# Sketched attention and SwiGLU on one core: one chunk made plain, one weight third differenced later, two chunks summed on VectorE

## The chip, the cores and the metric

One core of one Trainium2 chip runs the whole program. The metric is the time of one execution in microseconds; the kernel before was run three times. TensorE, VectorE, ScalarE, GpSimd and SyncE are PE, DVE, ACT, POOL and SP in the profile; "PEld" is TensorE's weight loading, which overlaps its products. Each engine, and each engine's queue of DMA issues, works strictly in the order in which the program lists its instructions.

## What is computed

```
phi(x) = outer product of (S1 x) and (S2 x), 8 x 8 = 64 features      q, k, v: 4 batches x 4 heads x 1088 x 32
num = phi(q) . sum_s phi(k) v^T        den = phi(q) . sum_s phi(k) + 1e-6
x = num / den, heads side by side                                     4352 tokens x 128
g = x @ w_gate;  val = x @ w_val;  out = (silu(g) * val) @ w_out      d_ff = 1536, in 12 chunks of 128
```

## The kernel before, in words

**Tiles.** The tokens stand as columns (`xT`, 128 x 4352) and are cut into blocks: three of 384, 320 and 384 columns for the first batch, and then `line`, the seven later blocks 3 to 9: six of 480 columns and a last one of 384. A *unit* is one block with one of the 12 chunks of d_ff: the products with `w_gate` and `w_val`, the Silu, and the product of the two, which gives a "hidden" tile. After that the unit's hidden tile is multiplied by its chunk of `w_out` and added up over the chunks in PSUM (`down`).

**The later blocks.** The loop over `y` (L1427) runs through 84 units; unit `y` is chunk `y % 12` of block `line[y // 12]`. Below, (m, j) is chunk j of `line[m]`, so unit 12 is (1, 0) and unit 26 is (2, 2). In each turn of the loop `start_unit` is called for unit y+1 (L1006: two matmuls into a pair of PSUM banks, and L1009: ACT rescales the pair), then `finish_unit` for unit y (L1018 and L1019: four more matmuls into its pair; L1021: ACT's Silu; L1026: DVE's multiply, which writes the hidden tile and gives the pair of banks back), and then `down` for an older unit. There are three pairs, so the start of unit y+3 cannot write the second bank of its pair until L1026 of unit y has read it.

**Plain and fine chunks.** `down` has two forms. A *plain* chunk is one fp32 matmul (L1094), which the profile shows as two passes. A *fine* chunk, listed in `DOWN` (L904), is three fp32r matmuls (L1086, L1088, L1089) with three parts of the hidden tile, `h1`, `h0` and `hd`, and three parts of `w_out`, `w1`, `wb` and `wd` (the tile `dparts`). `cut_hidden` (L960) makes the parts of the hidden tile: `h1` a scaled and rounded copy (ACT, L975, one unit later), `h0` the rest (DVE, L983, two units later), `hd` their sum. For a *carried* chunk `hd` is made by DMA: SP copies `h1` into it (L977) and POOL issues a DMA that adds `h0` to it (L987). For the others DVE adds (L989). All chunks of `line[:3]` in `DOWN` are carried; of the blocks 6 to 8 the odd ones; of the last none. The parts live in sets of three buffers, taken from a list and given back by `down`.

**The parts of w_out.** `cut_down` (L925) makes `dparts` in three thirds of the ten chunks 1 to 10: a is chunks 1 to 3, b is 4 to 6, c is 7 to 10. DVE's last step, `differ` (L941), gives `wd`; for c it is queued behind unit 12. Only L1086 reads `wd`.

**Order by hand.** `add_to(before, y, f)` and `add_to(behind, y, f)` put a step into the program ahead of unit y's four finishing matmuls, or behind its L1026. Nothing is rescheduled afterwards. The list `mine` (L1079) holds a block's fine chunks; behind the last of them `copy_out` (L1107) lets ACT copy the fine sums out of PSUM (L1112) into one of the five `sg` buffers; `put_together` adds both sums (L1122), and `store` transposes them (L1146) for the output.

**Attention of the later batches** is spread over the same units. Around units 9 to 19 it is batch 2's query step: DVE's L382 (last key features, tile `late`), L757, L760, L762, L763 and L764 (the denominators), then L382 and L774 in turn; POOL's five adds L552 (`zs`, the sums of the key features), which read what L382 wrote; SP's small copies L742; ACT's loads L178. POOL also makes `x0` of the next block (L884).

Of the kernel before, what the change touches and what calls it, by code (L numbers as in the profile page):

```python
# [19 lines left out]
def kernel(  # L20
# [53 lines left out]
    LAST = len(blocks) - 1  # L74
# [758 lines left out]
    def whole(ap):  # L833
        return ap.bitcast(FP32)
# [66 lines left out]

    line = list(range(HEAD, len(blocks)))
    FINE = range(1, NCH - 1)
    DOWN = [(line[0], j) for j in (2, 3, 4, 5, 6, 9)]  # L904
    DOWN += [(line[1], j) for j in (6, 7, 8, 9, 10)]
    DOWN += [(line[2], j) for j in (1, 2, 4, 5, 6, 8, 9, 10)]
    DOWN += [(i, j) for i in line[3:6] for j in FINE]
    DOWN += [(LAST, j) for j in range(1, 9)]
    down_parts = {}
# [6 lines left out]
    before, behind = {}, {}  # L916

    def add_to(where, y, f):
        where.setdefault(y, []).append(f)

    def now(where, y):
        for f in where.pop(y, ()):
            f()

    def cut_down():  # L925

        n = len(FINE)
        parts = const.tile([P, 3, n, D], F32R, tag="room", name="dparts", bufs=1)
        w1, wb, wd = (parts[:, k] for k in range(3))
        down_parts.update(w1=w1, wb=wb, wd=wd)  # L930

        def high(c):
            nc.scalar.activation(w1[:, c], wo[:, FINE[0] :][:, c], AF.Copy, scale=CUT)

        def left(c):
            nc.gpsimd.tensor_tensor(
                out=wb[:, c], in0=whole(w1[:, c]), in1=wo[:, FINE[0] :][:, c], op=ALU.subtract
            )

        def differ(c):  # L940
            nc.vector.scalar_tensor_tensor(  # L941
                out=wd[:, c], in0=whole(wb[:, c]), scalar=BETA, in1=whole(w1[:, c]),
                op0=ALU.mult, op1=ALU.add,
            )

        a, b, c = slice(0, 3), slice(3, 6), slice(6, n)
        high(a)
        yield
        high(b)
        yield  # L950
        high(c)
        add_to(behind, 2, lambda: left(a))
        add_to(behind, 2, lambda: left(b))
        add_to(behind, 5, lambda: differ(a))
        add_to(behind, 6, lambda: differ(b))
        add_to(behind, 2, lambda: left(c))
        add_to(behind, 12, lambda: differ(c))
        yield

    def cut_hidden(y, i, j):  # L960

        while len(h_free) < 3:
            y0, tags = h_more.pop(0)
            assert y >= y0
            for tag, n in tags:
                t = const.tile([P, n, WB], F32R, tag=tag, name="h" + tag, bufs=1)
                h_free.extend(t[:, k, :] for k in range(n))
        n = SPLIT if i == LAST else blocks[i][1]
        h_sets[i, j] = [h_free.pop(0) for _ in range(3)]
        h1, h0, hd = h_parts[i, j] = [x[:, 0:n] for x in h_sets[i, j]]  # L970
        h = hidden[i, j][:, 0:n]
        small = -CUT / BETA
        carried = i in line[:3] or i != LAST and j % 2
        if carried or j % 2:
            add_to(behind, y + 1, lambda: nc.scalar.activation(h1, h, AF.Copy, scale=small))  # L975
        if carried:
            add_to(behind, y + 1, lambda: nc.sync.dma_start(out=whole(hd), in_=whole(h1)))  # L977
        if not carried and j % 2 == 0:
            high = lambda: nc.vector.tensor_scalar(h1, h, small, None, op0=ALU.mult)
            before.setdefault(y + 1, []).insert(0, high)  # L980

        def rest():
            nc.vector.scalar_tensor_tensor(  # L983
                out=h0, in0=whole(h1), scalar=BETA, in1=h, op0=ALU.mult, op1=ALU.add
            )
            if carried:
                nc.gpsimd.dma_start(out=hd, in_=h0, accum_op=ALU.add)  # L987
            else:
                nc.vector.tensor_tensor(out=hd, in0=whole(h1), in1=whole(h0), op=ALU.add)  # L989

        add_to(before, y + 2, rest)
# [19 lines left out]
    def finish_unit(i, j, y=None):  # L1011
        n = blocks[i][1]
        x1, x0, _ = (x[:, 0:n] for x in x_parts[i])
        ps = sums_of.pop((i, j))
        now(before, y)
        for k, w in enumerate((wg, wv)):
            w1, wb = (w_parts[id(w), j // 3][t][:, j % 3, :] for t in range(2))
            nc.tensor.matmul(ps[:, k], w1, x1, start=False, stop=False, skip_group_check=True)  # L1018
            nc.tensor.matmul(ps[:, k], wb, x0, start=False, stop=True, skip_group_check=True)  # L1019
        sg = fpool.tile([P, WB], FP32, tag="sg", name="sg", bufs=5)[:, 0:n]  # L1020
        nc.scalar.activation(sg, ps[:, 0], AF.Silu, scale=WHOLE)  # L1021
        slot_of[i, j] = slots.pop(0)
        hj = slot_of[i, j]
        hidden[i, j] = hj
        todo.append((i, j))
        nc.vector.scalar_tensor_tensor(  # L1026
            out=hj[:, 0:n], in0=ps[:, 1], scalar=WHOLE, in1=sg, op0=ALU.mult, op1=ALU.mult
        )
        let_go((i, j))
        now(behind, y)  # L1030
        if (i, j) in DOWN:
            cut_hidden(y, i, j)
# [38 lines left out]
    def down(y=None):  # L1071
# [6 lines left out]
        made[i] = made.get(i, 0) + 1  # L1078
        mine = [c for c in range(NCH) if (i, c) in DOWN]  # L1079
        if mine and j == mine[0]:  # L1080
# [129 lines left out]
    c0, c1, aside = fpieces  # L1210
# [188 lines left out]
    while todo:  # L1399
        if len(todo) == 2:  # L1400
            start_unit(HEAD, 0)
        next_down()
        at(*steps_at.get(len(todo), ()))
        next(x_steps, None)
        if len(todo) == 7:
            parts_of(1)
            x_steps = cut_tokens(HEAD, nc.vector, soon=True)
            next(x_steps)
        if len(todo) == 6:
            down_steps = cut_down()  # L1410
        if len(todo) in (4, 5, 6):
            next(down_steps, None)
        if len(todo) in (2, 3, 4):
            parts_of(1)
# [77 lines left out]
```

## Time and profile before

| what | value |
|---|---|
| time of the kernel before, median of 3 runs | 276.21 us (275.74 to 276.25) |
| the profiled execution's own time | 276.19 us |
| its span, from first to last instruction | 274.5 us (1.69 us of the time lies around it) |
| DVE busy | 221.1 us (81%) |
| ACT busy | 197.6 us (72%) |
| POOL busy | 85.7 us (31%) |
| granted TensorE clock | 1.0 |
| DMA moved | 31.03 MB, mean 113 GB/s |

A row of the timeline gives the start and the duration in us, engine, line, operation, tiles and shape, and in brackets how long the engine had been idle before it and what released it. A row of the chain of waits gives start, duration, and the engine or DMA that held the end up in that stretch. In a table of windows each engine's busy time in the stretch is given, then the granted clock, the busy share of the DMA engines and GB/s.

### The profile page before, as it was taken

The page shows a single profiled execution, that of the slowest core. Times are in us where ns is not written, and L with a number is a line of the kernel's source. Part 1 is how long each engine was busy: PE and PEld are TensorE (multiplying, and loading weights), DVE is VectorE, ACT ScalarE, POOL GpSimd, SP SyncE. Part 2 cuts the span into 40 slices and gives each one's busy share as a digit, 9 for nine tenths or more (in the row PEclk, how much of TensorE's full clock was granted, in tenths as well). Part 3 has the DMA queues.
Part 4 walks back from the last instruction along what each step waited for, and adds up shares of the span by engine and source line. Part 5 has one row for each costly group of instructions (what it writes and reads, how often), then busy time and mean ns, then how long its engine had stood idle before and what let it go on. Part 6 is the DMA issues. An engine that isn't in the chain of part 4 may idle for free.

```text
span 274.5 us, 5978 instructions
## 1 busy us (share of the span) xinstructions
PE 266.5 (97%) x2208; PEld 203.1 (74%) x2208; DVE 221.1 (81%) x423; ACT 197.6 (72%) x353; POOL 85.7 (31%) x108
## 2 busy tenths in 40 slices
PE   7899999999999999998999999999999999999994
PEld 6645566666785777876677878767888888789994
DVE  3997988989788798999766788668968986996981
ACT  2468666462686789866678998768979888897860
POOL 3313422149340593273042143313213221221000
PEclk9999999999999999999999999999999999999999
DMA  6573197121331057751137688954464472565021
GB/s 194 169 218 89 46 264 207 61 104 56 68 87 24 4 145 184 150 132 31 38 90 174 124 203 170 193 109 108 91 121 114 101 160 63 125 125 110 2 36 30
DMA packets 35933, 31.03 MB, mean 113 GB/s; under 512 B 20928, under 2 KB 33984, under 8 KB 35904
## 3 DMA queue, kind: packets, MB, share of 16 engines
q1 hardware_dynamic: 29776, 21.64, 27.7%
q0 software_dynamic: 4896, 8.36, 17.8%
q10 hardware_dynamic: 1232, 0.66, 0.9%
q8 instruction: 17, 0.28, 0.4%
q14 instruction: 12, 0.10, 0.1%
HBM read 11.41 MB, written 2.23 MB: 50 GB/s over the span
## 4 chain that ended last, share of the span: by engine, by line
PE 86%; DVE 6%; DMA 3%; ACT 2%; issue 1%; ACTq 0%; SPq 0%
PE PS L1094 15%; PE PS L1006 13%; PE PS L1018 13%; PE PS L1019 12%; PE PS L1042 12%; PE PS L1086 4%; PE PS L1089 4%; PE PS L1088 4%; PE PS L359 2%; PE PS L347 2%; DMA hkT<-hextra 2%; PE PS L792 2%; PE PS L393 2%; DMA kld<-in_k_dram 2%; DVE hbuf L1026 1%
## 5 line engine op out<-in xcount | busy, mean ns | idle before, releaser
L1009 ACT ACTIVATE PS<-PS 128x960 f32<-128x960 f32 (+1 forms) x90 | 83.3, 925 | 26.7 <-PE PS L1006 25.9
L1026 DVE SCALAR_TENSOR_TENSOR hbuf<-PS,sg 128x480 f32<-128x480 f32 (+1 forms) x81 | 51.9, 640 | 25.8 <-ACT sg L1021 23.2
L1021 ACT ACTIVATE sg<-PS 128x480 f32<-128x480 f32 (+1 forms) x90 | 49.7, 552 | 2.2 <-PE PS L1019 1.9
L1094 PE MATMUL PS<-hbuf,wo 128*128 128x480 f32 (+3 forms) x88 | 36.9, 510 | 0.0
L1006 PE MATMUL PS<-xd,wd 128*128 128x480 f32 (+1 forms) x90 | 33.7, 375 | 1.0 <-DVE hbuf L1026 1.0
L1006 PE MATMUL PS<-xd,graw 128*128 128x480 f32 (+1 forms) x69 | 34.1, 494 | 0.0
L1019 PE MATMUL PS<-x,wb 128*128 128x480 f32 (+1 forms) x90 | 33.5, 372 | 0.0
L1018 PE MATMUL PS<-x,w 128*128 128x480 f32 (+1 forms) x90 | 33.4, 371 | 0.0
L1019 PE MATMUL PS<-x,graw 128*128 128x480 f32 (+1 forms) x69 | 25.6, 371 | 0.0
L1042 PE MATMUL PS<-xT,wg 128*128 128x384 f32 (+1 forms) x60 | 23.5, 473 | 0.1
L1042 PE MATMUL PS<-xT,wv 128*128 128x384 f32 (+1 forms) x60 | 23.2, 468 | 0.3 <-DVE wv L288 0.3
L1006 PEld LDWEIGHTS PS<-xd,wd 128*128 128x128 f32 x90 | 16.9, 188 | 8.5 <-issue 2.1
L1046 ACT ACTIVATE sg<-PS 128x384 f32<-128x384 f32 (+1 forms) x24 | 11.2, 468 | 13.1 <-PE PS L1042 12.3
L1094 PEld LDWEIGHTS PS<-hbuf,wo 128*128 128x128 f32 x88 | 16.3, 189 | 4.0 <-issue 0.4
L1018 PEld LDWEIGHTS PS<-x,w 128*128 128x128 f32 x90 | 16.9, 188 | 2.2
L1019 PEld LDWEIGHTS PS<-x,wb 128*128 128x128 f32 x90 | 16.9, 188 | 2.1
L1018 PE MATMUL PS<-x,graw 128*128 128x480 f32 (+1 forms) x48 | 18.0, 376 | 0.0
L1006 PEld LDWEIGHTS PS<-xd,graw 128*128 128x128 f32 x69 | 13.0, 188 | 6.1 <-ACT PS L1009 2.6
L1042 PEld LDWEIGHTS PS<-xT,wv 128*128 128x128 f32 x60 | 11.2, 190 | 7.4 <-DVE hbuf L1057 0.8
L1042 PEld LDWEIGHTS PS<-xT,wg 128*128 128x128 f32 x60 | 10.9, 190 | 7.7 <-issue 1.1
L1018 PE MATMUL PS<-x,gphq 128*128 128x480 f32 (+1 forms) x42 | 16.0, 380 | 0.1
L1019 PEld LDWEIGHTS PS<-x,graw 128*128 128x128 f32 x69 | 12.9, 188 | 1.4
(287 smaller groups left out, 576.3 us busy)
## 6 DMA issues: line engine op xcount, KB each, us to landing
kld<-in_k_dram SPq DMA_DIRECT2D x4, 544.0 KB, 4.3
qld<-in_q_dram SPq DMA_DIRECT2D x3, 544.0 KB, 5.9
raw<-in_moe_w_out_dram SPq DMA_DIRECT2D x4, 384.0 KB, 5.5
vld<-in_v_dram SPq DMA_DIRECT2D x9, 144.0 KB, 5.2
hwg<-hwg POOLq DMA_DIRECT2D x5, 240.0 KB, 3.2
hextra<-hextra POOLq DMA_DIRECT2D x5, 240.0 KB, 3.4
raw<-in_moe_w_gate_dram SPq DMA_DIRECT2D x3, 384.0 KB, 3.5
raw<-in_moe_w_val_dram SPq DMA_DIRECT2D x3, 384.0 KB, 3.6
```

Source lines behind the costliest of these rows:

```text
L1006: nc.tensor.matmul(ps[:, k], w_parts[id(w), j // 3][2][:, j % 3, :], xd, start=True, stop=True)
L1009: nc.scalar.activation(ps, ps, AF.Copy, scale=-1.0 / WHOLE)
L1018: nc.tensor.matmul(ps[:, k], w1, x1, start=False, stop=False, skip_group_check=True)
L1019: nc.tensor.matmul(ps[:, k], wb, x0, start=False, stop=True, skip_group_check=True)
L1021: nc.scalar.activation(sg, ps[:, 0], AF.Silu, scale=WHOLE)
L1026: nc.vector.scalar_tensor_tensor(out=hj[:, 0:n], in0=ps[:, 1], scalar=WHOLE, in1=sg, op0=ALU.mult, op1=ALU.mult)
L1042: nc.tensor.matmul(o[:, 0:n], w[:, j, :], xT[:, t0 : t0 + n], start=True, stop=True)
L1046: nc.scalar.activation(sg[:, 0:n], g[:, 0:n], AF.Silu)
L1086: nc.tensor.matmul(acc[i][:, 0:n], wd, hd, **sides)
L1088: nc.tensor.matmul(p, w1, h1, start=(j == mine[0]), stop=False)
L1089: nc.tensor.matmul(p, wb, h0, start=False, stop=(j == mine[-1]))
L1094: nc.tensor.matmul(acc[i][:, 0:n], wo[:, j, :], hidden[i, j][:, 0:n], **sides)
```

## The change

Three edits. Chunk (0, 9) is no longer fine: its down is one plain matmul, and its `h1`, `h0` and `hd`, with one SP copy and one POOL DMA, are not made. `differ(c)` moves from behind unit 12 to behind unit 21. For (2, 2) and (2, 8), `hd` is made by DVE's add L989 in place of SP's copy and POOL's DMA; their `h1` stays on ACT.

```diff
-    DOWN = [(line[0], j) for j in (2, 3, 4, 5, 6, 9)]
+    DOWN = [(line[0], j) for j in (2, 3, 4, 5, 6)]
...
-        add_to(behind, 12, lambda: differ(c))
+        add_to(behind, 21, lambda: differ(c))
...
-        carried = i in line[:3] or i != LAST and j % 2
-        if carried or j % 2:
+        carried = i in line[:3] and (i, j) not in [(line[2], 2), (line[2], 8)] or i in line[3:-1] and j % 2
+        aside = carried or j % 2 or i in line[:3]
+        if aside:
             add_to(behind, y + 1, lambda: nc.scalar.activation(h1, h, AF.Copy, scale=small))
         if carried:
             add_to(behind, y + 1, lambda: nc.sync.dma_start(out=whole(hd), in_=whole(h1)))
-        if not carried and j % 2 == 0:
+        if not aside:
             high = lambda: nc.vector.tensor_scalar(h1, h, small, None, op0=ALU.mult)
             before.setdefault(y + 1, []).insert(0, high)
```

The lists of instructions of both programs, laid side by side, differ in this, beside the names of the buffer sets: on PE three fine matmuls give way to one plain one; on DVE one L983 is gone, L941 stands behind L1026 of unit 21, and two L989 are new, each behind its chunk's L983; on ACT one L975 is gone and block 3's L1112 stands three units earlier (the last fine chunk of the block is now 6); on POOL three L987 are gone, the first of them from directly ahead of the five L552; on SP three L977 are gone. The line numbers behind L973 grow by one.

## The prediction

> **What bounds the kernel now.** I read the page's busy shares first, then the chain of waits in order of time, then the rows around each break in it. The shares and the chain's summary:
>
> ```profile
> PE 266.5 (97%) x2208; PEld 203.1 (74%) x2208; DVE 221.1 (81%) x423; ACT 197.6 (72%) x353; POOL 85.7 (31%) x108
> ...
> PE 86%; DVE 6%; DMA 3%; ACT 2%; issue 1%; ACTq 0%; SPq 0%
> ```
>
> TensorE sets the end; a microsecond counts only where PE does more, or waits. So I look for pieces of the chain that are not PE's. Behind the start-up there are two that the change touches:
>
> ```profile
> 119.03 0.66 DVE hbuf L1026
> 119.68 1.39 DVE dparts L941
> 121.07 1.21 DVE den L762
> 122.30 0.39 DVE den L763
> 122.75 1.07 issue
> 123.82 0.66 DVE hbuf L1026
> ...
> 169.11 4.61 DMA hkT<-hextra
> ```
>
> The first is DVE's queue between L1026 of unit 12 (119.03) and of unit 13 (123.82), with L941, the moved step, in it. The second is a POOL DMA, the `hd` of (2, 6), whose landing PE waits for. What they cost, from PE's weight loads (start, duration):
>
> ```profile
> 120.58 0.19 PEld L1006 LDWEIGHTS PS<-xd,graw 128*128 128x128 f32 x1 [0.21 <-ACT PS L1009]
> ...
> 122.69 0.19 PEld L1006 LDWEIGHTS PS<-xd,graw 128*128 128x128 f32 x1 [0.21 <-ACT PS L1009]
> 124.51 0.19 PEld L1006 LDWEIGHTS PS<-xd,wd 128*128 128x128 f32 x1 [1.63 <-DVE hbuf L1026]
> ...
> 126.15 0.19 PEld L1006 LDWEIGHTS PS<-xd,graw 128*128 128x128 f32 x1
> ```
>
> **Stall 1.** These L1006 with `graw` open units 15, 16 and 17. From 122.69 to 126.15 is 3.46 us; the same stretch, a unit behind a plain chunk that ends in a fine one, takes 2.15 undisturbed (161.87 to 164.02). So stall 1 is 3.46 - 2.15 = 1.31, less than the 1.63 of the bracket, since PE was still working off the plain chunk. **Stall 2.** The step from 172.01 to 174.31 is 2.30; its neighbour, 170.03 to 172.01, is 1.98: 0.32.
>
> **Why stall 1 is so long.** DVE's L941 took 1.47 us; its two shorter sisters took 0.55 for 384 columns, so 512 should take 0.73. L762 took 1.27 against 0.17 elsewhere, L764 1.18 against 0.46. POOL's rows show what stood beside them:
>
> ```profile
> 118.34 0.86 POOL L987 DMA_DIRECT2D hwg<-hkld  x1 [3.44 <-DVE dot L757]
> 118.91 1.61 POOL L552 TENSOR_TENSOR zs<-late 128x512 f32<-128x512 f32 x1
> 120.59 2.99 POOL L552 TENSOR_TENSOR zs<-zs,late 128x512 f32<-128x512 f32 x2
> ```
>
> L941 ended 0.55 behind the first add's end, and L762 and L764 end likewise just behind an add: these DVE steps stand still while POOL adds. L1026 (PSUM operand, 0.66 at 119.03) and L763 (0.38) ran beside the adds unstretched. And the adds themselves are late because POOL's L987 ahead of them, for (0, 9), waited 3.44 us.
>
> **The change, part by part.**
>
> *(0, 9) plain, price.* Starts of units behind fine chunks are 1.95 to 1.97 apart (chain rows 152.31, 154.26, 156.23), behind plain ones 2.12 (160.31, 162.43): +0.16. It is paid in full, PE has no slack there. ACT loses an L975 (0.61), DVE an L983 (0.65), SP a 0.49 issue, POOL the waiting L987. L1112 (0.58) moves up behind Silu of unit 13, which ends at 120.94; the next L1009 starts at 121.62, so it just fits, and if not, that L1009 ends 0.7 before PE needs it. Nothing.
>
> *(0, 9) and L941, gain.* I walk DVE's queue through the new order, with PE's times of before. Unit 16's second load, due 0.41 behind its first (as 120.58 to 120.99), needs L1026 of unit 13 done by 123.10; it was done at 124.46. The adds now wait only for POOL's previous L987 (ends 114.90) and for DVE's L382 (second of three, ends 114.4; one more for the next add, one at 115.68 for the third). I take adds of 1.3 to 1.4 us (the shortest elsewhere is 1.27) and 0.75 for the half ones, the two engines taking turns: add 1 from 115.0 to 116.4; L382 116.4 to 117.1; add 2 to 118.4, with L1026 of unit 11 beside it at 117.1; L757 118.4 to 118.85; add 3 to 120.15, beside it L760 to 119.3 and L1026 of unit 12 to 119.95; L762 to 120.3; add 4 to 121.05, L763 beside it; L764 to 121.5; add 5 beside L1026 of unit 13, 121.5 to 122.15. That is 0.95 before 123.10. With the adds' recorded lengths (1.61, 1.50, 1.50, 0.82) it ends at 122.9, still in time. Behind it L382 (0.95) and L1026 of unit 14 end near 124.5, due at about 125.2; later L1026 follow PE again. So all of stall 1 goes: -1.31. Bounds: nothing gained, or 1.9 lost (third rival).
>
> *L941 behind unit 21.* 0.73 us; it goes ahead of L889, L1146 and L983, which now end at 144.61, and L1026 of unit 22 comes at 146.11 after 1.50 idle. These end at 145.35; the L987 behind that L983 was issued at 145.62, held by SP's copy. Its first reader, (1, 7)'s L1086, comes at 151.5. Nothing; without that idle time up to 0.73.
>
> *Two L989, and four transfers gone.* L989 took 0.657 in all its full-width rows. Its places are ahead of L1026 of unit 28 (1.07 idle) and of unit 34 (0.83 idle): both fit, 0.4 and 0.2 left. Nothing; without this cover up to 0.66 each, of which PE sees what exceeds some 1.2 (unit 28's L1026 ends at 159.20, its reader's load comes at 160.37). The transfers matter in a full stretch (PE, PEld, DVE, ACT, POOL, then the clock, the DMA share, GB/s):
>
> ```profile
> 166.00:170.00 4.00, 4.00 (x18) 3.15 (x17) 3.44 (x6) 3.31 (x6) 1.43 (x2) 1.00 1.05 193
> 170.00:174.00 4.00, 3.94 (x18) 3.06 (x18) 3.22 (x5) 3.89 (x7) 0.86 (x1) 1.00 0.96 210
> ```
>
> The DMA engines are full. There the `hd` of (2, 6), issued at 169.11, took 4.6 us; others take 3.2 to 3.6 when it is quieter. PE wanted it at 173.33, so 4.2 would do. (2, 8)'s copy, issued at 168.76 and 3.7 us on its way, ran beside it all the time and is gone. One of about five such transfers less makes 4.6 some 3.7: -0.32. Bounds: nothing, or 0.32.
>
> **Sum.** -1.31 - 0.32 + 0.16 = -1.47. The profiled execution took 276.19 (span 274.5), 0.02 below the median of 276.21: 276.19 - 1.47 = **274.7**, span near 273.0.
>
> **A rule that speaks against it.** The Trainium skill, "SBUF — State Buffer", section "Who interferes with whom", says that a DVE instruction with two SBUF inputs contends with a GpSimd one that reads SBUF, that issue order decides, and that the loser blocks for the whole instruction. L941 shows it here, 1.47 against 0.73. The rule counts the new L989 too. By my rows L989 of (2, 2) runs from 157.47 to 158.13, before POOL's L884 (158.50, 1.54 us). Were L884 first, that L989 would end near 160.7, L1026 of unit 28 near 161.4, 1.0 behind its reader, and the sum would be -0.5.
>
> **Rivals.**
>
> 1. *Only stall 1 goes.* 276.19 - 1.31 + 0.16 = 275.0. For it: the stretch stays near full with three outputs and two more transfers in it. Against it: 0.4 us is enough.
> 2. *The adds keep half of stall 1,* because they start no earlier than now (something else holds POOL): 274.7 + 0.65 = 275.4, at worst 276.0. For it: most waits on POOL are put down to steps that can't be the cause, so what held it is not certain. Against it: the L987 is the only waiting step ahead.
> 3. *Slower: POOL's adds take DVE's turn everywhere.* They now start beside L382 and meet L757 as well. If each add and each DVE step stood one behind the other, from 115.03 on, 6.8 us of adds and 4.6 us of DVE (0.68 + 0.66 + 0.45 + 0.45 + 0.66 + 0.17 + 0.38 + 0.46 + 0.66) end at 126.4, 1.9 later than now: 276.19 + 1.9 + 0.16 - 0.32 = 277.9. It makes the kernel slower from where L1026 of unit 13 ends after about 125.2 (124.46 - 0.16 + 0.32 + 0.55). Against it: L1026, L760 and L763 do not wait for adds.
> 4. *It doesn't do what it says:* something else holds PE at both places, such as L1112 in its new place; only the plain chunk's price stays: 276.2 to 276.4.
>
> **Chances.** Forecast 0.56, rival 1 0.14, rival 2 0.11, rival 3 0.10, rival 4 0.09. A measurement of this kernel tells about 0.2%, 0.55 us, from no change. Faster takes the forecast, rival 1 and some 0.07 of rival 2: 0.77. The same takes the rest of rival 2 and rival 4: 0.13. Slower is rival 3: 0.10. The range takes in forecast, rival 1 and rival 2 (0.81), from 274.2 (0.5 more than reckoned) to 276.0.
>
> **What would show it.** L1026 of unit 13 within 3.2 us of unit 12's (now 4.8), and no wait of PE for it; the first L552 directly behind the L987 of (0, 6), near 115; L941 near 0.7 us behind unit 21; the DMA wait at L1086 of (2, 6) gone; units of (0, 9)'s down 2.1 apart. A stretched L757 or L382 and a late L1026 of unit 13 would speak for rivals 2 and 3; a new wait of PE for L1026 of units 22, 28 or 34 would show covers that I took as safe.

## The result, and the profile after

The changed kernel takes 274.69 us (median of 6 runs, 274.35 to 274.81) against 276.12 us before (6 runs, 275.74 to 276.25): ratio 0.9949, 95% interval 0.9936 to 0.9962, or 1.43 us less. The forecast was 274.7. Its profiled execution took 274.57 us (span 272.9). Behind L973 all line numbers are one higher than before: the multiply is L1027, the weight loads of a start are L1007, POOL's accumulating DMA is L988.

The page's busy shares and the chain's summary, as shown of before:

```profile
PE 266.4 (98%) x2207; PEld 203.0 (74%) x2207; DVE 220.7 (81%) x424; ACT 197.0 (72%) x352; POOL 82.7 (30%) x105
...
PE 92%; DVE 3%; DMA 2%; ACT 1%; issue 1%; SPq 0%; ACTq 0%
```

The busy times have hardly moved; the chain's share of PE went from 86% to 92%. What went was waiting. DVE's timeline where stall 1 was:

```profile
118.72 0.66 DVE L1027 SCALAR_TENSOR_TENSOR hbuf<-PS,sg 128x480 f32<-128x480 f32 x1 [0.29 <-ACT sg L1022]
119.30 0.66 DVE L762 TENSOR_SCALAR den<-den 128x36 f32<-128x36 f32 x1
119.99 0.38 DVE L763 RECIPROCAL den<-den 128x36 f32<-128x36 f32 x1
120.40 0.63 DVE L764 TENSOR_TENSOR qab<-qab,den 128x288 f32<-128x288 f32 x1
120.96 0.64 DVE L1027 SCALAR_TENSOR_TENSOR hbuf<-PS,sg 128x480 f32<-128x480 f32 x1
```

From the multiply of unit 12 to that of unit 13 is now 2.24 us (before 4.79), L762 takes 0.66 (1.27) and L764 0.63 (1.18). POOL's timeline says why: the adds follow the DMA of (0, 6) at once, and the last of them ends at 120.72.

```profile
113.42 0.86 POOL L988 DMA_DIRECT2D hkT<-hkT  x1 [1.00 <-PE PS L1007]
114.34 1.58 POOL L552 TENSOR_TENSOR zs<-late 128x512 f32<-128x512 f32 x1
115.99 3.11 POOL L552 TENSOR_TENSOR zs<-zs,late 128x512 f32<-128x512 f32 x2
119.18 0.73 POOL L552 TENSOR_TENSOR zs<-zs 128x256 f32<-128x256 f32 x1
120.00 0.72 POOL L552 TENSOR_TENSOR zs<-zs,late 128x256 f32<-128x256 f32 x1
```

PE's weight loads with `graw` that open units 15, 16 and 17 start at 120.27, 122.38 and 124.49, 2.11 apart as behind any plain chunk; the bracket of 1.63 is gone.

In the stretch of stall 2 (windows: PE, PEld, DVE, ACT, POOL, clock, DMA share, GB/s; the work in them stands 1.5 us further on than in the same windows of before) the DMA engines come free sooner, 0.55 of the second window against 0.96:

```profile
166.00:170.00 4.00, 4.00 (x18) 3.14 (x17) 3.81 (x7) 3.78 (x7) 0.86 (x1) 1.00 0.99 153
170.00:174.00 4.00, 4.00 (x21) 3.44 (x20) 3.29 (x6) 3.44 (x6) 0.86 (x1) 1.00 0.55 158
```

The three added DVE steps stand in their covers. L941 takes 0.68 at 141.36, and 0.92 of idle time is left before the multiply of unit 22. The two sums on DVE's timeline, with the idle time that is left (0.36, 0.16) in the brackets of the multiplies:

```profile
156.06 0.66 DVE L990 TENSOR_TENSOR hwg<-hkld,hwg 128x480 fp32r<-128x480 f32 x1
157.09 0.66 DVE L1027 SCALAR_TENSOR_TENSOR hbuf<-PS,sg 128x480 f32<-128x480 f32 x1 [0.36 <-ACT sg L1022]
...
168.07 0.66 DVE L990 TENSOR_TENSOR hkT<-hextra 128x480 fp32r<-128x480 f32 x1
168.89 0.66 DVE L1027 SCALAR_TENSOR_TENSOR hbuf<-PS,sg 128x480 f32<-128x480 f32 x1 [0.16 <-ACT sg L1022]
```

One wait is new. PE's load for the `down` of (5, 9), the last chunk with a DMA-made `hd`, stands 2.08 behind its neighbour, where 1.71 is the step before:

```profile
249.38 0.19 PEld L1087 LDWEIGHTS PS<-hwv,dparts 128*128 128x128 f32 x1
251.46 0.19 PEld L1087 LDWEIGHTS PS<-hsoon,dparts 128*128 128x128 f32 x1 [0.36 <-DMA hsoon<-hwv]
```

**Where the time went, by stretches.** The first weight load of each `down` is a mark that every trace has. Between some of them I take differences, in every profiled execution but the last experiment's (us, one execution a row):

| kernel | start to (0,6) | (0,6) to (1,0): stall 1 | (2,4) to (2,7): stall 2 | (5,6) to (5,11) | last chunk to end | span |
|---|---|---|---|---|---|---|
| before | 118.02 | 14.94 | 6.23 | 8.57 | 6.27 | 274.5 |
| changed | 117.70 | 13.79 | 5.87 | 8.83 | 6.26 | 272.9 |
| changed_again | 117.82 | 13.80 | 5.87 | 8.96 | 6.25 | 273.1 |
| plain_only | 117.81 | 13.79 | 6.08 | 8.82 | 6.41 | 273.3 |
| third_early | 117.77 | 13.64 | 6.03 | 8.65 | 6.25 | 272.8 |
| no_adds | 117.68 | 13.63 | 6.09 | 8.57 | 6.25 | 272.7 |
| sums_only | 117.94 | 14.97 | 5.91 | 8.82 | 5.84 | 274.0 |
| sum_2_2 | 118.00 | 14.98 | 5.90 | 8.57 | 6.41 | 274.3 |
| sum_2_8 | 117.99 | 14.95 | 6.26 | 8.57 | 6.43 | 274.7 |
| third_early_sums | 117.91 | 13.64 | 5.91 | 8.69 | 5.84 | 272.5 |
| third_early_sums_b | 117.75 | 13.63 | 5.90 | 9.18 | 5.84 | 272.8 |
| third_early_sums3 | 118.03 | 13.64 | 5.91 | 8.57 | 6.24 | 272.8 |
| changed_sum_5_9 | 117.78 | 13.79 | 5.87 | 8.55 | 6.45 | 272.9 |

The stretches left out, (1,0) to (2,4), (2,7) to (5,6) and (5,11) to the last chunk, stay within 36.37 to 36.43, 72.17 to 72.21 and 11.81 to 11.85. So between the two profiles the span fell by 0.32 ahead of the change, 1.15 at stall 1 and 0.36 at stall 2, and rose by 0.26 at (5, 9): 1.6 with the small rest.

### The profile page after: what moved, and what is told of

The parts are those of the page before. It is cut to its first block, busy times and chain, and to the rows that moved or that the text cites. A ratio compares the mean times of both kernels' runs of the same rounds, so it can differ in the third digit from the quotient of the medians.

```text
span 272.9 us, 5961 instructions
## 1 busy us (share of the span) xinstructions
PE 266.4 (98%) x2207; PEld 203.0 (74%) x2207; DVE 220.7 (81%) x424; ACT 197.0 (72%) x352; POOL 82.7 (30%) x105
## 4 chain that ended last, share of the span: by engine, by line
PE 92%; DVE 3%; DMA 2%; ACT 1%; issue 1%; SPq 0%; ACTq 0%
PE PS L1095 16%; PE PS L1019 14%; PE PS L1007 14%; PE PS L1020 14%; PE PS L1043 12%; PE PS L1087 4%; PE PS L1090 4%; PE PS L1089 4%; PE PS L359 2%; PE PS L347 2%; PE PS L792 2%; PE PS L393 2%; DMA kld<-in_k_dram 2%; PE PS L1133 1%; PE PS L502 1%; PE PS L450 1%
## 5 line engine op out<-in xcount | busy, mean ns | idle before, releaser
L1010 ACT ACTIVATE PS<-PS 128x960 f32<-128x960 f32 (+1 forms) x90 | 83.3, 925 | 26.0 <-PE PS L1007 25.3
L1027 DVE SCALAR_TENSOR_TENSOR hbuf<-PS,sg 128x480 f32<-128x480 f32 (+1 forms) x81 | 51.9, 641 | 24.6 <-ACT sg L1022 22.4
L1095 PE MATMUL PS<-hbuf,wo 128*128 128x480 f32 (+3 forms) x90 | 37.9, 511 | 0.0
L1007 PE MATMUL PS<-xd,graw 128*128 128x480 f32 (+1 forms) x69 | 34.4, 499 | 0.0
L1007 PE MATMUL PS<-xd,wd 128*128 128x480 f32 (+1 forms) x90 | 33.5, 373 | 0.0
L1007 PEld LDWEIGHTS PS<-xd,wd 128*128 128x128 f32 x90 | 16.9, 188 | 7.3 <-issue 2.6
L1007 PEld LDWEIGHTS PS<-xd,graw 128*128 128x128 f32 x69 | 13.0, 188 | 6.2 <-ACT PS L1010 2.8
```

Of the source, the lines that this page charges most:

```text
L1007: nc.tensor.matmul(ps[:, k], w_parts[id(w), j // 3][2][:, j % 3, :], xd, start=True, stop=True)
L1010: nc.scalar.activation(ps, ps, AF.Copy, scale=-1.0 / WHOLE)
L1027: nc.vector.scalar_tensor_tensor(out=hj[:, 0:n], in0=ps[:, 1], scalar=WHOLE, in1=sg, op0=ALU.mult, op1=ALU.mult)
L1095: nc.tensor.matmul(acc[i][:, 0:n], wo[:, j, :], hidden[i, j][:, 0:n], **sides)
```

## The experiments

Theory T: POOL's adds stop DVE's SBUF steps, and unit 13's multiply is late because the adds come late (behind the DMA of (0, 9)) *and* L941 takes one turn more among them; take away either, and all of stall 1 goes. The third edit takes away stall 2. The rivals stand with each run.

### plain_only

```diff
-    DOWN = [(line[0], j) for j in (2, 3, 4, 5, 6, 9)]
+    DOWN = [(line[0], j) for j in (2, 3, 4, 5, 6)]
```

> The kernel before with the first edit alone: chunk (0, 9) plain; L941 stays behind unit 12 and all carried chunks stay carried. Theory T (two causes, either removed is enough: POOL's adds are late behind the L987 of (0, 9), and L941 takes one more turn among them): without that L987 the adds start near 115 and are nearly over when L941 comes; L941 loses one turn at most, L1026 of unit 13 ends near 122.3 (profile's time, deadline 122.8 to 123.1), so all of stall 1 goes. 276.12 - 1.31 + 0.16 = 275.0. Rival R1 (each edit carries a part of it, both are needed): L1026 of unit 13 ends near 123.6, 0.5 to 0.7 of the stall stays, 275.5 to 275.7. Rival R2 (the move of L941 was all of the gain): nothing but the plain chunk's price, 276.3.

275.08 us (5 runs, 274.51 to 275.46), before 276.03; ratio 0.9959 (0.9947 to 0.9971). Theory T holds: with L941 still behind unit 12, stall 1's stretch is 13.79, as in the changed kernel. DVE's and POOL's timelines show one turn each way:

```profile
119.40 1.13 DVE L941 SCALAR_TENSOR_TENSOR dparts<-dparts 128x512 fp32r<-128x512 f32 x1
120.45 0.71 DVE L762 TENSOR_SCALAR den<-den 128x36 f32<-128x36 f32 x1
```

```profile
119.24 0.74 POOL L552 TENSOR_TENSOR zs<-zs 128x256 f32<-128x256 f32 x1
120.05 1.06 POOL L552 TENSOR_TENSOR zs<-zs,late 128x256 f32<-128x256 f32 x1
```

L941 ends at 120.53, 0.55 behind the add that ended at 119.98; the next add then takes 1.06 in place of 0.72, until 121.11, 0.58 behind L941; and L762, with 36 columns, ends at 121.16, just behind that add. L764, with no add left, takes 0.46. The multiply of unit 13 ends at 122.63, in time.

### third_early

```diff
-        add_to(behind, 12, lambda: differ(c))
+        add_to(behind, 5, lambda: differ(c))
```

> The kernel before with one edit that the change does not have: the third L941 is queued behind unit 5 with the first, where DVE has 1.01 us idle before L1026 of unit 7; (0, 9) stays fine, so POOL's adds stay late (about 118.9). Theory T: L762 and L764 still wait for an add each, but one turn is gone; L1026 of unit 13 ends near 123.0, at its deadline, and 1.2 to 1.3 of stall 1 goes: 276.12 - 1.25 = 274.9. Rival R1 (the late adds are a cause of their own): L1026 of unit 13 ends near 123.7 and half of the stall stays, 275.5. Rival R2 of the plain run (the move of L941 is all of it) gives 274.8 as well and is told apart by the plain run. Rival R3: the fuller DVE queue behind unit 5 holds up L1026 of unit 7, a new stall of up to 0.5, 275.4.

274.74 us (12 runs, 274.51 to 276.73); ratio 0.9954 (0.9938 to 0.9971). All of stall 1 goes again, 13.64, and without a plain chunk. Here the adds are as late as before (the first at 118.68), and DVE pays for two turns in place of three:

```profile
119.36 0.98 DVE L762 TENSOR_SCALAR den<-den 128x36 f32<-128x36 f32 x1
...
120.79 1.19 DVE L764 TENSOR_TENSOR qab<-qab,den 128x288 f32<-128x288 f32 x1
121.90 0.64 DVE L1026 SCALAR_TENSOR_TENSOR hbuf<-PS,sg 128x480 f32<-128x480 f32 x1
```

So the first two edits are not two halves of stall 1: each alone is enough. Rivals R1, R2 and R3 fall. In the changed kernel the plain chunk is needed all the same: with L941 behind unit 21 a fine (0, 9) would read a `wd` that isn't written yet. Its price, 13.79 against 13.64, buys a later place for L941, and behind unit 5 there was one for nothing.

### no_adds

```diff
+        if bare: return s[:, 0, :], [lambda: nc.gpsimd.memset(s[:, 0, :], 1.0)]
...
-                zs, sums = feature_sums(phk)
+                zs, sums = feature_sums(phk, True)
```

> The kernel before with POOL's five adds L552 around unit 13 left out, with all else as it was, L941 behind unit 12 and the L987 of (0, 9) too: a memset stands in their place, so the sums of key features of the last batch are not computed. Theory T (DVE's steps there stand still while POOL adds): L941 takes 0.73 (1.47 with the adds), L762 0.17 (1.27), L764 0.46 (1.18), the multiply of unit 13 ends near 121.5 and stall 1 is gone: 276.05 - 1.31 = 274.7. Rival X (they were long for another reason, such as the DMA traffic or their own tiles): the three keep their lengths and the time stays at 276.05.

274.51 us (4 runs, 274.25 to 275.3); ratio 0.9945 (0.9928 to 0.9962). The same DVE steps, in the same order and at the same place, with no add beside them:

```profile
119.26 0.68 DVE L941 SCALAR_TENSOR_TENSOR dparts<-dparts 128x512 fp32r<-128x512 f32 x1
119.86 0.17 DVE L762 TENSOR_SCALAR den<-den 128x36 f32<-128x36 f32 x1
...
120.48 0.46 DVE L764 TENSOR_TENSOR qab<-qab,den 128x288 f32<-128x288 f32 x1
```

The same three in the kernel before:

```profile
119.60 1.47 DVE L941 SCALAR_TENSOR_TENSOR dparts<-dparts 128x512 fp32r<-128x512 f32 x1
120.99 1.27 DVE L762 TENSOR_SCALAR den<-den 128x36 f32<-128x36 f32 x1
...
122.71 1.18 DVE L764 TENSOR_TENSOR qab<-qab,den 128x288 f32<-128x288 f32 x1
```

They take 0.68, 0.17 and 0.46 in place of 1.47, 1.27 and 1.18; L763 takes 0.38 in both. That the adds stop them is shown. Rival X falls.

### sums_only, sum_2_2 and sum_2_8

`sums_only` is the third edit alone; the other two are halves of it:

```diff
-        carried = i in line[:3] or i != LAST and j % 2
+        carried = i in line[:3] and (i, j) not in [(line[2], 2), (line[2], 8)] or i in line[3:-1] and j % 2
...
+        carried = i in line[:3] and (i, j) not in [(line[2], 2)] or i in line[3:-1] and j % 2
...
+        carried = i in line[:3] and (i, j) not in [(line[2], 8)] or i in line[3:-1] and j % 2
```

> The kernel before with the third edit alone: hd of (2, 2) and (2, 8) by DVE's L990 in place of SP's copy and POOL's DMA. Theory T: only stall 2 goes, 276.12 - 0.32 = 275.8, with the wait of L1087 of (2, 6) gone. Rival R4 (the DMA stretch stays full without them, and in the changed kernel the 0.33 came from something else): 276.1, the wait stays. Rival R5 (four transfers less change who comes when further back, as the new wait of the changed kernel at (5, 9) suggests): 276.1 with the first wait gone and a new one of 0.3 at (5, 9).

> The kernel before with hd of (2, 2) alone on DVE; (2, 8) stays carried. In the run with both, stall 2 went because the accumulating DMA of (2, 6) was issued 1.04 us earlier (168.07 against 169.11) and landed in 3.5 in place of 4.6. Theory V (the transfers ahead of it, (2, 2)'s, hold up the chain of (2, 4) and (2, 5), so the earlier issue is what counts): (2, 6)'s DMA is issued near 168.1, the step from (2, 6) to (2, 7) is 1.97, time 275.8. Rival W, the recorded step of the prediction ((2, 8)'s copy ran beside it and made the landing long): issued at 169.1 and landing 4.6 as before, step 2.30, time 276.05.

> The kernel before with hd of (2, 8) alone on DVE; (2, 2) stays carried. Theory V: (2, 6)'s DMA is still issued near 169.1; its landing may be shorter, but if it stays above 4.2 the stall stays, step 2.0 to 2.3, time 275.9 to 276.05. Rival W: issued at 169.1, landing 3.5 to 3.7, step 1.97, time 275.8: stall 2 gone by this transfer alone.

`sums_only`: 275.78 us (11 runs), before 276.03, ratio 0.9987 (0.9979 to 0.9996). `sum_2_2`: 276.20 (11 runs), before 276.05, ratio 1.0 (0.9989 to 1.0011). `sum_2_8`: 276.21 (12 runs), ratio 1.0004 (0.9996 to 1.0013). The times of the halves tell nothing, 0.3 us being about what the interval allows; the stretches do. With (2, 2) on DVE, alone or not, (2,4) to (2,7) takes 5.87 to 5.91 in eight executions; with (2, 2) carried 6.03 to 6.26 in five. In `sum_2_8` the stall stands a chunk earlier: in its chain of waits the accumulating DMA of (2, 5) takes 5.91 (before 5.43), and PE waits 0.49 for that one.

```profile
165.83 5.91 DMA hextra<-hextra
```

That run went neither theory's way in full. The DMA of (2, 6) was issued at 167.75, not near 169.1, since SP's copy ahead of it landed in 2.36 in place of 3.70. Up to that copy the program is that of before, so this is a difference between executions and no effect of the edit.

With (2, 2) alone POOL's timeline has the DMAs of (2, 5) and (2, 6) 2.35 apart, the second at 168.12; before they were 3.40 apart (165.71 and 169.11), at the same place of PE's work (171.36 and 171.39 for the load of (2, 5)).

```profile
165.77 0.86 POOL L988 DMA_DIRECT2D hextra<-hextra  x1 [1.36 <-DVE hbuf L1027]
168.12 0.86 POOL L988 DMA_DIRECT2D hkT<-hextra  x1 [1.49 <-DVE phT L774]
```

W, my recorded step, falls: in `sum_2_2` the copy of (2, 8) still runs beside the DMA of (2, 6), from 168.79 for 3.40, and that DMA lands in 3.33 all the same; in `sum_2_8`, without the copy, it took 5.44. Theory V stands for the place, by eight executions against five: what counted was the transfer pair ahead of the three. SP's copy of (2, 4), the next behind that pair, landed in 2.3 in all eight and in 3.35 in `plain_only`. V's time for `sum_2_2`, 275.8, was not measured: the stretch is 0.33 shorter than before, but the part behind the last chunk 0.14 longer, and the median is 276.20. Of rival R5, `sums_only` has the wait at (5, 9), 0.25. It gained in its profile by the end part, 5.84 against 6.27, of which more below.

### third_early_sums, third_early_sums3 and changed_sum_5_9

The first is `third_early` with `sums_only`; it was run again as `third_early_sums_b`, beside the changed kernel. The second puts (5, 9) on DVE too; the third does that to the changed kernel.

```diff
+        carried = i in line[:3] or i in line[3:-1] and j % 2
+        carried = carried and (i, j) not in [(line[2], 2), (line[2], 8), (line[5], 9)]
```

> Third L941 behind unit 5 and the two L990, with (0, 9) left fine: the changed kernel without the plain chunk. Theory T: stall 1 goes without the plain chunk, its 0.16 is not paid, stall 2 goes: 276.12 - 1.25 - 0.32 = 274.55, 0.1 to 0.2 below the changed kernel. Rival R1: 275.2, half a microsecond above it.

> Third L941 behind unit 5, (0, 9) fine, hd on DVE for (2, 2), (2, 8) and now (5, 9) too, whose accumulating DMA PE waited for in the changed kernel (step 2.08 in place of 1.71) and a little in the run with the third early and the two sums (1.92). DVE has over 1.0 us idle there, an add takes 0.66. Theory: that wait goes, 274.31 - 0.2 = 274.1. Rival: the add meets the narrow units at the end, whose own steps are on DVE, and comes late itself: 274.3 or above.

> The changed kernel once more, beside its two variants. In its first profile PE waited for the accumulating DMA of (5, 9): the stretch from its 73rd to its last narrow step took 8.83 where the kernel before has 8.57, 0.26 more, and SP's copy ahead of it landed in 3.8 in place of 3.3. Theory L (the margin of that transfer is about nothing, so it is a matter of a few tenths of landing time in each execution): the copy lands in 3.0 to 3.9 and the stretch takes 8.57 to 8.85; time 274.5 to 274.8. Rival M (the edits themselves make it late): the copy takes 3.8 again and the stretch 8.83.

> The changed kernel with hd of (5, 9) on DVE too, so that its transfer cannot make PE wait: the stretch takes 8.57. If that wait is in most executions of the changed kernel, its time is 0.26 below the changed kernel's of the same chip, 274.4 against 274.7; if it is in few, the two are the same.

> Third L941 behind unit 5, the two sums on DVE, (0, 9) fine, beside the changed kernel on one chip. Theory T: the changed kernel pays 0.15 for a plain chunk that buys nothing once L941 is out of the crowd, so this one is 0.15 to 0.4 below it: 274.3 to 274.55 against 274.7. Rival: no difference.

| kernel | us, median | range, runs | ratio, 95% interval |
|---|---|---|---|
| third_early_sums | 274.31 | 274.10 to 275.12, 6 | 0.9939 (0.9926 to 0.9952) |
| third_early_sums_b | 274.46 | 274.16 to 274.98, 5 | 0.9944 (0.9932 to 0.9957) |
| third_early_sums3 | 274.57 | 274.48 to 274.75, 5 | 0.9943 (0.9932 to 0.9955) |
| changed_again | 274.62 | 274.38 to 274.81, 5 | 0.9949 (0.9936 to 0.9961) |
| changed_sum_5_9 | 274.61 | 274.54 to 274.91, 5 | 0.9952 (0.9938 to 0.9966) |

With L941 behind unit 5, (0, 9) fine and the two sums, the kernel has the lowest medians of all, 0.16 below the changed kernel on the same chip (274.46 against 274.62) and 0.4 below it in runs that were not beside it, as expected in sign; the intervals overlap, and one of the reasons is not the one I gave (the end part, 5.84). For the wait at (5, 9) the record speaks for rival M rather than theory L: in the changed kernel SP's copy landed in 3.82 and 3.93 and PE lost 0.26 and 0.39, and the two other kernels that hold the first edit and this transfer have it as well, `plain_only` with 3.80 and 0.25, `sum_beside_add` with 3.84 and 0.30. Without the first edit it differs: 0 in `sum_2_2`, 0.25 in `sums_only`, and in two executions of one program, `third_early_sums` and `third_early_sums_b`, the copy landed in 3.58 and 2.53. In the second PE lost nothing at (5, 9), but 0.6 at (5, 7), whose accumulating DMA took 4.2. How a plain (0, 9) acts so much later in the program is not shown; the parts of the chunks behind it lie in other buffers. Putting (5, 9) on DVE does take the wait away (8.57 and 8.55), and yet both kernels gained nothing by it: in their profiles the part behind the last chunk is longer than in the kernels without that edit, 6.24 against 5.84 and 6.45 against 6.25 and 6.26. My expectations of 274.1 and 274.4 were wrong by 0.5 and 0.2.

### sum_beside_add

```diff
+            elif (i, j) == (line[2], 2):
+                add_to(behind, y + 2, lambda: nc.vector.tensor_tensor(out=hd, in0=whole(h1), in1=whole(h0), op=ALU.add))
```

> The changed kernel with the DVE sum of (2, 2) moved behind unit 28, ahead of a transpose L774, so that it is queued while POOL's L884 runs (156.94 to 158.49). Theory T (a DVE step with SBUF operands stands still until the POOL step ends): it is recorded with about 1.45 us in place of 0.66, ending near 159.1, and the multiply of unit 29 starts near 160.1 in place of 158.7. Rival (only the adds L552 block): 0.66, and the multiply of unit 29 near 159.3. The time is 274.7 to 275.0 in either case.

275.62 us (one run), 1.0 above the changed kernel's 274.62 on that chip. DVE's timeline (the multiply is L1029 here), and POOL's:

```profile
157.27 0.66 DVE L1029 SCALAR_TENSOR_TENSOR hbuf<-PS,sg 128x480 f32<-128x480 f32 x1 [1.06 <-ACT sg L1024]
157.85 2.25 DVE L990 TENSOR_TENSOR hwg<-hkld,hwg 128x480 fp32r<-128x480 f32 x1
...
160.92 0.61 DVE L1029 SCALAR_TENSOR_TENSOR hbuf<-PS,sg 128x480 f32<-128x480 f32 x1
```

```profile
158.03 1.54 POOL L884 TENSOR_TENSOR x<-xT,x 128x480 fp32r<-128x480 f32 x1
```

The same add that takes 0.66 elsewhere takes 2.25 and ends 0.53 behind L884's end: it stood still for the whole of it. The adds L552 are not special. PE then waited 0.83 and 0.47 for two of the multiplies behind it. I had expected the block, but shorter (1.45, since L884 began 1.1 later here than in the changed kernel) and without a price. Of the loss 0.86 stands in the stretch from (1, 0) to (2, 4), 37.25 in place of 36.39. It is about the 1.0 that the prediction reckoned, under its "rule that speaks against it", for a sum that meets L884; a place 1.8 us earlier in DVE's queue is all that keeps the changed kernel from it.

## Why the prediction was right, point by point

- *Stall 1, 1.31.* Right: 1.31 (14.94 to 13.63) with the adds left out, 1.30 with L941 early, and 1.15 with the plain chunk paid. Not seen: that either edit alone does it, so the walk through DVE's queue was nowhere near its limit.
- *The walk.* The adds began where it put them, behind the DMA of (0, 6): at 114.34, which is 114.65 in the time of before, where it had 115.0. The multiply of unit 13 came 2.24 behind unit 12's; the walk had 2.2 (119.3 to 121.5). Rival 3's marks were there, L382 of 1.08 in place of 0.68 and L757 of 0.60 in place of 0.45, but each step paid once, and the adds were over by 120.7. Rivals 1, 2 and 4 fall with the stretches 13.79 and 5.87.
- *Plain chunk, +0.16.* Right: 13.79 less 13.64, 0.15. L1113 in its new place (120.52, 0.58) delayed nothing: ACT's L1010 behind it started at 121.31. Not reckoned: the wait at (5, 9), 0.25 to 0.39 in all four executions that hold the first edit and that transfer.
- *L941 and two sums at nothing.* Right, with 0.92, 0.36 and 0.16 left of covers of 1.50, 1.07 and 0.83. The Trainium skill, "SBUF — State Buffer", section "Who interferes with whom", says that a DVE instruction with two SBUF inputs contends with a GpSimd instruction that reads SBUF; `no_adds` and `sum_beside_add` agree, the second with 2.25 us in place of 0.66. L762 has one tensor as input and was stopped as well, 1.27 with the adds and 0.17 without.
- *Stall 2, 0.32.* The size is right (6.23 to 5.87), but this is the step that failed: "(2, 8)'s copy ... ran beside it all the time and is gone. One of about five such transfers less makes 4.6 some 3.7". That copy landed at 172.46, so it did not run beside the DMA to its end at 173.72, and with the copy in place, in `sum_2_2`, the DMA landed in 3.33. Without the copy alone the stretch stays at 6.26; without (2, 2)'s pair it is 5.90: the DMA of (2, 4) is issued 0.9 earlier there, that of (2, 5) lands in 4.5 in place of 5.4, and that of (2, 6) is issued 1.0 earlier. Part of the 0.32 goes with stall 1, too: 6.03 to 6.09 in the three executions that lose stall 1 and keep the pair.
- *The sum.* -1.47 against a measured -1.43 of the medians. In the two profiles it is -1.6, and there two pieces that I had not reckoned stand against each other. The 0.32 ahead of (0, 6) is no effect of the change: `no_adds`, which has the program of before up to there, starts 0.34 earlier than before. The 0.26 at (5, 9) belongs to the changed kernel, which had it each time. Stretch by stretch the edits gave 1.15 + 0.36 - 0.26 = 1.25. So agreement to 0.04 is partly luck; to 0.3 it is the mechanism.

## What to carry to other kernels

When two engines share a path, count the steps of one that stand among the other's, not their lengths: L762, with 36 columns, lost 1.10 us, and L941, with 512, lost 0.79. Before two edits are priced as a sum, ask of each whether it would do alone; here the one that costs 0.15, and more at (5, 9), was needed only for the place chosen for the other. And in a chain of equal transfers with no slack, look at the ones ahead of the late one first: here it was a pair ahead that counted, not the copy beside it.

## What the hardware showed that I had not expected

- DVE and POOL took strict turns when both had work queued: in `plain_only` add, L941, add, L762, each starting where the other ended, and POOL's add was stretched by DVE's L941 (1.06 against 0.72) as DVE's was by POOL's. In `sum_beside_add` DVE's record even starts 0.18 ahead of POOL's, and POOL went first; recorded starts overlap the step ahead by about 0.1, so who was really issued first can't be read there.
- An accumulating DMA of 240 KB landed in anything from 3.1 to 5.9 us, and SP's copy of the same size in 2.2 to 4.4, the same copy of one program in 2.5 and 3.6.
- The part behind the last chunk, with the same work in all kernels, goes with how many chunks' transfers were taken out earlier: 6.25 to 6.27 with none, 6.41 to 6.43 with one, 5.84 with two, 6.24 to 6.26 with three, 6.45 with four, and within 0.01 when a kernel is repeated. The last four DMAs are issued at the same place in all and land, where the trace shows it, in 1.4 to 1.6 us, so the difference lies behind them. The traces show where: SyncE closes the program (L1487 of before) with nine waits for semaphores, each 0.06 to 0.09 behind the one before it when nothing holds it. In the kernel before the second of them is held, to 4.94 behind the last chunk's mark, and seven follow, to 5.40; in `sums_only` it is the eighth, to 4.91, and one follows, to 4.98. The difference is as large as the smaller edits here. Why another of the nine is held stays open; no run was made on it.
